# Attention and two mixture-of-experts layers in one kernel: two weight halves are split at other places, and the last block is scaled by one engine

## The chip, the cores and the metric

The kernel runs on one core of a Trainium2 chip. The metric is the device time of one execution in microseconds (us), the median of several runs. The engines are named as the profile names them: PE is TensorE's matmuls and PEld its weight loads, DVE is VectorE, ACT is ScalarE, POOL is GpSimd, SP is the queue that issues most of the loads.

## What is computed

A decayed linear attention gives 1536 rows of 512. These go through a first layer of eight experts, in which each row is used only if a skip score is positive and whose result is added to the row, and then through a second layer of eight experts with a capacity. Each layer picks one expert for each row by the largest logit, applies two matrices with a ReLU between them, and scales by the softmax weight:

```python
def reference(**kwargs):
    ...
    attn_out = _attn_ref(**attn_kwargs)
    B, H, S, D = attn_out.shape
    x = np.ascontiguousarray(attn_out.transpose(0, 2, 1, 3)).reshape(B * S, H * D)
    x = _moe_ref(x=x, **moe_kwargs)
    return _moe2_ref(x=x, **moe2_kwargs)

def _moe_ref(x, w_skip, w_gate, w1, w2):
    ...
        h = np.maximum(xc[mask] @ w1[e], 0.0)
        y[mask] = gate_w[mask, None] * (h @ w2[e])
    out[do_compute] = xc + y

def _moe2_ref(x, w_gate, w1, w2, capacity):
    ...
    h = np.maximum(np.einsum('ecd,edf->ecf', disp, w1), 0.0)
    y = np.einsum('ecf,efd->ecd', h, w2)
    ...
            out[i] = gate_w[i] * y[expert_idx[i], pos[i]]
```

## The kernel before

**Products and weights.** A product of float32 matrices is made from three products of rounded parts: a tensor x is split into hi, x rounded to the type fp32r, and lo = x − hi, rounded likewise; hi·hi, hi·lo and lo·hi are summed (`mm3`, `mm3s`, lines 803 to 811). The weights come from DRAM as float32, in chunks of 1 MB (half a matrix of an expert), into five raw buffers named big. A chunk is split in two halves of 128x1024: for each half ScalarE makes hi (line 258) and VectorE lo (line 261). With the second half the raw buffer goes back to a list of free ones, and the next chunk can be loaded into it from SP's queue (line 219); SP's load waits for the last reader of the buffer, which is VectorE's subtraction. Weights of the first layer are w1a and w2a, of the second w1b and w2b.

**How the order is set.** The program's order on each engine is the order in which the Python code emits it. Generators emit a layer piece by piece. Between the pieces the code calls `step_side`, which first lets the routing generators take a step and then calls `pump(1, pieces[0])`: `pump` raises a counter of turns, emits up to `pieces[0]` weight halves (each with its ScalarE and its VectorE instruction), if a loaded chunk and a place for it are there, and then issues the loads for which buffers are free. So `pieces[0]` says how many halves are split at a step.

**The first layer and its picks.** For each expert e the code emits layer 1 (`layer1`: products into s, ReLU at line 834 into h), turns h by transposes on TensorE (line 782) with the rounding on ScalarE (line 387, hTh) and the remainder on VectorE (line 388, hTl), and runs layer 2 of the expert before it (`layer2`, products into o). `result` (line 866) scales that expert's accumulator and adds the row on VectorE, which makes its rows for the second layer ("row"). The rows are then routed by `route_b`, for the experts 0 to 5 in couples, for 6 and for 7 alone: transposes on TensorE (line 887), logits (lines 892 and 898), the pick on VectorE (`pick`: the maximum mx at line 307, d, t, tm and the mask m at line 323, with ScalarE's exponential ex at line 315), ranks by two products of the mask (lines 335 and 336), slot and one-hot row on VectorE (lines 918, 920 and 924), and eight or four products into the slot table tab (line 349). The third couple is that of experts 4 and 5.

**Between the layers.** Beside layer 1 of the second layer's expert 0 the rows of expert 7 are routed (the generator `last`; its steps are called at i = 2, 4, 5, 8 and 12 of the loop from line 1084). Then VectorE casts the slot table to indices (line 1094, ids_b), and POOL issues five indirect gathers of 128 rows each by these indices (`load_block`, line 371). The first of them, block (0, 1), is turned on TensorE at line 782 amid layer 2 of expert 0.

**The second layer and the end.** Expert 0 has its two blocks one at a time, experts 1 to 7 two blocks of 128 rows as a pair (`pair_layer1`, `pair_layer2`). `emit_out` scales a block's accumulator by the softmax weight into y, and POOL scatters y to the output rows (line 941). For the very last block the work of the scaling is shared: ScalarE takes columns 0 to 255 (line 936) and VectorE columns 256 to 511 (line 938). All other blocks are scaled by ScalarE alone.

Of the kernel before, what the change touches and what calls it, by code (L numbers as in the profile page):

```python
# [11 lines left out]
ACTF = mybir.ActivationFunctionType  # L12
ALU = mybir.AluOpType
# [3 lines left out]
NT, DM, E, FF = B * S, H * D, 8, 1024  # L17
# [7 lines left out]
GCOL, IDCOL = DM, DM + 2  # L25
# [16 lines left out]
def kernel(  # L42
# [12 lines left out]
    nc = tc.nc  # L55
# [136 lines left out]
    def whole(kind, e, j):  # L192

        return kind == "w2a" and e in (1, 3) and j == 1
# [72 lines left out]
    def used(key, h):  # L267
        if key not in whole_keys:
            w_free.append((count["turn"] + 2, held.pop((key, h))))
        elif h:  # L270
            raw_free.append((0, held.pop(key)))
# [4 lines left out]
    def pump(n, pieces):  # L276

        count["turn"] += 1
        for _ in range(pieces):
            if not splitting:  # L280
                if not ready():
                    break
                splitting.append(split_half(n))
            try:
                next(splitting[0])
            except StopIteration:
                splitting.clear()
        load_w()
# [77 lines left out]
    def gather(at, n=None, t=None):  # L366

        n = n or done[0]
        if t is None:
            t = xs_free.pop(0)  # L370
        nc.gpsimd.indirect_dma_start(
            out=t, out_offset=None, in_=table[0:n, :], in_offset=bass.IndirectOffsetOnAxis(ap=at, axis=0),
            bounds_check=n - 1, oob_is_err=False,
        )
        return t
# [386 lines left out]
    def psum(tag="t", bufs=3):  # L762
        return ps.tile([128, 512], F32, tag=tag, bufs=bufs, name=tag)
# [43 lines left out]
    def mm3s(acc, pairs, first, last):  # L807

        todo = [(a[0], w[i]) for a, w in pairs for i in range(2)] + [(a[1], w[0]) for a, w in pairs]
        for i, (a, w) in enumerate(todo):  # L810
            nc.tensor.matmul(out=acc, lhsT=a, rhs=w, start=first and i == 0, stop=last and i == len(todo) - 1)  # L811
            if i % 2 and i < len(todo) - 1:
                yield

    def at_k(parts, *ix):
        return tuple(t[(slice(None),) + ix] for t in parts)

    def layer1(x, kind, e, parts=None, fine=False):

        h = m_p.tile([128, FF], F32, tag="h", name="h", bufs=1)  # L820
        for j in range(2):
            acc = psum("s", 2)
            for k in (0, 2):
                w = wt[kind, e, j][k // 2]
                for _ in mm3s(acc, [(at_k(x, k + i), at_k(w, i)) for i in range(2)], k == 0, k == 2):
                    if fine:
                        yield
                if done_with(kind, e):
                    used((kind, e, j), k // 2)
                if not k:  # L830
                    if j and parts is not None:
                        parts.append(turned(h, 0, "hT"))
                    yield
            nc.scalar.activation(out=h[:, 512 * j:512 * j + 512], in_=acc, func=ACTF.Relu)
            yield
        return h

    def layer2(hT, kind, e):
        acc = psum("o", 2)
        for k in range(0, FT, 2):  # L840
            w = wt[kind, e, k // 4]
            a = hT[k // 4]
            h, k0 = k % 4 // 2, k % 4
            if whole(kind, e, k // 4):
                for i in (k0, k0 + 1):
                    nc.tensor.matmul(out=acc, lhsT=a[0][:, i, :], rhs=w[:, i, :], start=k + i == 0, stop=k == FT - 2 and i == 3)  # L846
            else:
                for _ in mm3s(acc, [(at_k(a, k0 + i), at_k(w[h], i)) for i in range(2)], k == 0, k == FT - 2):
                    pass
            if done_with(kind, e):  # L850
                used((kind, e, k // 4), h)
            yield
        return acc
# [4 lines left out]
    def done_with(kind, e):  # L858
        if (kind, e) not in (("w1b", 0), ("w2b", 0)):
            return True  # L860
        return uses.get(kind, 0) > 0
# [68 lines left out]
            to_slots(where[i], rhs[:, i], 8, 8)  # L930
        yield

    def emit_out(xs, acc, shared=False):
        y = m_p.tile([128, DM], F32, tag="y", name="y")
        n = DM // 2 if shared else DM
        nc.scalar.activation(out=y[:, 0:n], in_=acc[:, 0:n], func=ACTF.Copy, scale=xs[:, GCOL + 1:GCOL + 2])  # L936
        if shared:
            nc.vector.tensor_scalar(out=y[:, n:DM], in0=acc[:, n:DM], scalar1=xs[:, GCOL + 1:GCOL + 2], scalar2=None, op0=ALU.mult)
        ix = sm.tile([128, 1], I32, tag="ixo", name="ixo")
        nc.gpsimd.tensor_scalar(out=ix, in0=xs[:, IDCOL:IDCOL + 1], scalar1=4096.0, scalar2=None, op0=ALU.add)  # L940
        new = nc.gpsimd.indirect_dma_start(  # L941
            out=out[:, :], out_offset=bass.IndirectOffsetOnAxis(ap=ix, axis=0), in_=y, in_offset=None,
            bounds_check=NT - 1, oob_is_err=False,
        )
        for old in written:
            tc.declare_no_dep(new.ins, old.ins, reason="rows of other tokens")
        written.append(new)
        if xs is not a0:
            xs_free.append(xs)
# [18 lines left out]
    pieces = [1]  # L968
# [9 lines left out]
    def step_side():  # L978
        for g in list(side):
            try:  # L980
                next(g)
            except StopIteration:
                side.remove(g)
        pump(1, pieces[0])

    def run(gen):

        while True:
            try:
                next(gen)  # L990
            except StopIteration as stop:
                return stop.value
            step_side()
# [5 lines left out]
    def last_step(gen, n):  # L999

        for i in range(n):
            next(gen)
            if i < n - 1:
                step_side()
        try:
            next(gen)
        except StopIteration as stop:
            return stop.value
# [23 lines left out]
    acc = run(second)  # L1032
    then_route(0, acc)
    for e in range(1, E):
        first = layer1(x, "w1a", e)
        if e == 1:
            for _ in range(2):
                next(first)
                step_side()
            x = turned(xs1[2], 0, "x")  # L1040
        h = run(first)
        if e + 4 < E:
            xs1[e + 4] = gather(ids[:, e + 4:e + 5], 1 + NT)
        elif e == 4:
            gather(ids[:, 8:9], 1 + NT, a0)
        turn = split_T(h, FT, "hT", (True, not whole("w2a", e, 1)))
        if e > 1:
            second = layer2(hT.pop(e - 1), "w2a", e - 1)
            next(second)
            step_side()  # L1050
            site()
            x = turned(xs1[e + 1] if e + 1 < E else a0, 0, "x")
            if e == E - 1:

                for _ in range(2):
                    next(second)
                    step_side()
                    site()
                    next(turn)
            acc = last_step(second, FT // 2 - (3 if e == E - 1 else 1))  # L1060
            then_route(e - 1, acc, step_side)
        if e < E - 1:
            site()
        hT[e] = run(turn)
    side += sited
    second = layer2(hT.pop(E - 1), "w2a", E - 1)
    for i in range(FT // 2):
        next(second)
        pieces[0] = i < 2
        if i < FT // 2 - 1:  # L1070
            step_side()
    acc = run(second)
# [4 lines left out]
    xs2 = {(0, 0): a0}  # L1077

    def load_block(e, j):
        xs2[e, j] = gather(ids_b[:, 8 * j + e:8 * j + e + 1])  # L1080
# [3 lines left out]
    for i in range(1, 13):  # L1084
        next(first)
        if i % 3 == 0:
            step_side()
        if i in (2, 4, 5, 8, 12):
            next(last)
# [4 lines left out]
    nc.vector.tensor_copy(out=ids_b, in_=tab[:, 8:24])  # L1094
    for e, j in ((0, 1), (1, 0), (1, 1), (2, 0), (2, 1)):
        load_block(e, j)
    second = layer2(h0, "w2b", 0)
    next(second)
    h0.append(turned(h, 1, "hT"))
# [4 lines left out]
    acc = run(second)  # L1104
# [44 lines left out]
    def pair_layer2(hs, e):  # L1149
        acc = [psum("o", 2), psum("o", 2)]  # L1150
        for c in range(2):
            w = wt["w2b", e, c]
            for j in range(2):
                for k in range(4):
                    mm3(acc[j], at_k(hs[c], k, slice(128 * j, 128 * j + 128)), at_k(w[k // 2], k % 2), c + k == 0, c + k == 4)
                if c:
                    emit_out(xs2[e, j], acc[j], e == E - 1 and j > 0)
                for h in range(2 * j):
                    used(("w2b", e, c), h)
                step_side()  # L1160
# [11 lines left out]
    acc = run(second)  # L1172
# [207 lines left out]
```

## Time and profile before

| | |
|---|---|
| median of 3 runs (lowest, highest) | 386.19 us (384.45, 387.62) |
| the profiled execution | 386.53 us |
| its span in the profile | 384.5 us |
| PE busy | 370.6 us, 96% of the span |
| PEld busy | 313.4 us, 82% |
| DVE busy | 244.2 us, 64% |
| ACT busy | 214.0 us, 56% |
| POOL busy | 116.0 us, 30% |

A span begins with the first instruction and ends with the last event that the profiler saw; all times of day in this document are microseconds from the span's start. An engine's instructions run in its program's order. "Idle before" is the time that an engine stood still ahead of an instruction, and the name behind the arrow is what ended that. The matmuls are pipelined, one begins before the modelled end of the one ahead, so a PE wait can be read by the distance of starts as well as by the idle time.

### The profile page before, as it was taken

The numbers are of one execution on the slowest core, as the hardware profiler recorded it, in microseconds if no ns is written. First come the engines' busy times: TensorE is split into PE (matmuls) and PEld (weight loads), VectorE is DVE, ScalarE is ACT, GpSimd is POOL, SyncE is SP. The second block draws the span as 40 slices with busy tenths as digits, with TensorE's granted clock in tenths as the row PEclk, the third lists the DMA queues.
The fourth block names the chain that finished last, engine by engine and source line by source line (L and its number), as shares of the span: only waits on it lengthen the run. The fifth ranks groups of instructions, "written<-read, shape, count | busy, mean of one in ns | idle before, by whom it ended". The sixth has DMA issues, their size and how long they took to land.

```text
span 384.5 us, 6806 instructions
## 1 busy us (share of the span) xinstructions
PE 370.6 (96%) x2641; PEld 313.4 (82%) x2641; DVE 244.2 (64%) x402; ACT 214.0 (56%) x317; POOL 116.0 (30%) x185
## 2 busy tenths in 40 slices
PE   8999999699999999999999999999999999999992
PEld 4788887688867778886678998989989898998981
DVE  3557776649998889799626983646727476373200
ACT  1446554458979668796337773547536454562100
POOL 3677773274130040142252401305032040401102
PEclk9999999789999999999999999999999999999997
DMA  8999876499999999898835784956749387110101
GB/s 297 415 421 400 355 222 219 113 412 350 414 411 402 334 360 331 298 310 318 294 116 162 263 338 134 313 195 202 267 146 331 112 263 267 54 51 14 41 2 45
DMA packets 18944, 95.99 MB, mean 250 GB/s; under 512 B 3217, under 2 KB 3473, under 8 KB 9432
## 3 DMA queue, kind: packets, MB, share of 16 engines
q1 hardware_dynamic: 13012, 80.86, 57.0%
q0 software_dynamic: 3280, 9.76, 8.0%
q10 hardware_dynamic: 2612, 4.86, 3.4%
q8 instruction: 23, 0.38, 0.4%
q14 instruction: 17, 0.14, 0.1%
HBM read 87.03 MB, written 9.48 MB: 251 GB/s over the span
## 4 chain that ended last, share of the span: by engine, by line
PE 88%; DVE 5%; ACT 3%; issue 2%; DMA 1%; POOL 0%; POOLq 0%; DVEq 0%; ACTq 0%
PE s L811 14%; PE o L811 9%; PE s L805 7%; PE s L804 7%; PE s L803 7%; PE o L805 7%; PE o L803 7%; PE o L804 7%; PE m L691 3%; PE s L641 3%; DVE lo L261 3%; PE t L782 3%; PE m L682 3%; PE o L846 2%; PE t L1121 2%
## 5 line engine op out<-in xcount | busy, mean ns | idle before, releaser
L261 DVE TENSOR_TENSOR lo<-big,hi 128x1024 fp32r<-128x1024 f32 (+1 forms) x130 | 151.1, 1184 | 58.2 <-ACT hi L258 57.7
L258 ACT ACTIVATE hi<-big 128x1024 fp32r<-128x1024 f32 (+1 forms) x130 | 128.0, 1014 | 2.9 <-DMA big<-in_w1a_dram 1.2
L805 PE MATMUL s<-xh,lo 128*128 128x256 f32 x224 | 63.4, 283 | 0.0
L804 PE MATMUL s<-xl,hi 128*128 128x256 f32 x224 | 63.4, 283 | 0.0
L803 PE MATMUL s<-xh,hi 128*128 128x256 f32 x224 | 63.4, 283 | 0.0
L941 POOL DMA_INDIRECT out_dram<-y,ixo x16 | 18.6, 1165 | 138.4 <-ACT y L936 136.8
L803 PE MATMUL o<-hi,hTh 128*128 128x512 f32 x112 | 44.2, 394 | 0.0
L805 PE MATMUL o<-hi,hTl 128*128 128x512 f32 x112 | 43.6, 390 | 0.0
L804 PE MATMUL o<-lo,hTh 128*128 128x512 f32 x112 | 43.6, 389 | 0.0
L804 PEld LDWEIGHTS s<-xl,hi 128*128 128x128 f32 x224 | 43.0, 192 | 0.3
L803 PEld LDWEIGHTS s<-xh,hi 128*128 128x128 f32 x224 | 43.0, 192 | 0.3
L805 PEld LDWEIGHTS s<-xh,lo 128*128 128x128 f32 x224 | 43.0, 192 | 0.0
L1140 ACT ACTIVATE hTh<-s 128x512 fp32r<-128x512 f32 x28 | 16.8, 598 | 39.0 <-PE s L805 39.0
L1141 DVE SCALAR_TENSOR_TENSOR hTl<-s,hTh 128x512 fp32r<-128x512 f32 x28 | 19.3, 690 | 28.4 <-ACT hTh L1140 28.4
L936 ACT ACTIVATE y<-o,rowc 128x512 f32<-128x512 f32 (+1 forms) x15 | 10.1, 675 | 45.3 <-issue 29.3
L811 PE MATMUL s<-hi,xh 128*128 128x512 f32 x80 | 33.4, 417 | 0.7 <-DVE xl L388 0.7
L811 PE MATMUL s<-lo,xh 128*128 128x512 f32 x80 | 32.0, 400 | 0.0
L811 PE MATMUL o<-hi,hTh 128*128 128x512 f32 x72 | 29.7, 412 | 0.0
L811 PE MATMUL o<-lo,hTh 128*128 128x512 f32 x72 | 28.2, 391 | 0.0
L811 PE MATMUL s<-hi,xl 128*128 128x512 f32 x80 | 25.4, 400 | 0.0
L805 PEld LDWEIGHTS o<-hi,hTl 128*128 128x128 f32 x112 | 21.0, 188 | 4.5
L804 PEld LDWEIGHTS o<-lo,hTh 128*128 128x128 f32 x112 | 21.1, 188 | 4.2
(162 smaller groups left out, 601.6 us busy)
## 6 DMA issues: line engine op xcount, KB each, us to landing
big<-in_w1a_dram SPq DMA_DIRECT2D x16, 1024.0 KB, 6.9
big<-in_w2a_dram SPq DMA_DIRECT2D x16, 1024.0 KB, 7.2
big<-in_w1b_dram SPq DMA_DIRECT2D x16, 1024.0 KB, 5.1
big<-in_w2b_dram SPq DMA_DIRECT2D x16, 1024.0 KB, 5.8
qk<-in_qkv_dram SPq DMA_DIRECT2D x5, 1024.0 KB, 8.4
big<-in_qkv_dram SPq DMA_DIRECT2D x5, 1024.0 KB, 8.4
table<-rowc ACTq DMA_DIRECT2D x4, 516.0 KB, 7.1
table<-row ACTq DMA_DIRECT2D x3, 516.0 KB, 5.3
```

The costliest lines, as they stand in the source:

```text
L258: nc.scalar.activation(out=hi[:, k], in_=r3[:, k], func=ACTF.Copy)
L261: nc.vector.tensor_tensor(out=lo[:, k], in0=r3[:, k], in1=hi[:, k].bitcast(F32), op=ALU.subtract)
L641: nc.tensor.matmul(out=sa[j][:, 128 * r:128 * r + 128], lhsT=kk[64 * j:64 * j + 64, r, :], rhs=q[64 * j:64 * j + 64, r, :], start=True, st ...
L682: nc.tensor.matmul(out=o[:, 128 * r:128 * r + 128], lhsT=sbd[c % 2][:, b, r, :], rhs=q[:, r, :], start=r == 0, stop=False, skip_group_chec ...
L691: nc.tensor.matmul(out=o[64 * j:64 * j + 64, 128 * r:128 * r + 128], lhsT=v[:, b, 2 * r + j, :], rhs=pt[c, b][j][:, r, :], start=not c and ...
L803: nc.tensor.matmul(out=acc, lhsT=a[0], rhs=w[0], start=first, stop=False)
L804: nc.tensor.matmul(out=acc, lhsT=a[0], rhs=w[1], start=False, stop=False)
L805: nc.tensor.matmul(out=acc, lhsT=a[1], rhs=w[0], start=False, stop=last)
L811: nc.tensor.matmul(out=acc, lhsT=a, rhs=w, start=first and i == 0, stop=last and i == len(todo) - 1)
L941: new = nc.gpsimd.indirect_dma_start(out=out[:, :], out_offset=bass.IndirectOffsetOnAxis(ap=ix, axis=0), in_=y, in_offset=None, bounds_che ...
L1140: nc.scalar.activation(out=hi[:, g:g + 2, :], in_=acc, func=ACTF.Relu)
L1141: nc.vector.scalar_tensor_tensor(out=lo[:, g:g + 2, :], in0=acc, scalar=0.0, in1=hi[:, g:g + 2, :].bitcast(F32), op0=ALU.max, op1=ALU.subtract
```

## The change

Three edits. In the iteration of the last first-layer expert, the two steps ahead of the row of expert 6 split one half and none, where they split one each; the step right behind that row splits two, where it split one. In the loop over layer 2 of expert 7, the steps split one half only at i = 0, where they did at i = 0 and 1; the half left over is split at the step of i = 9 of the loop in which expert 7's rows are routed. The last block is scaled by ScalarE over all 512 columns. The number of halves is the same, and so is their sequence.

```diff
-    def emit_out(xs, acc, shared=False):
+    def emit_out(xs, acc):
         y = m_p.tile([128, DM], F32, tag="y", name="y")
-        n = DM // 2 if shared else DM
-        nc.scalar.activation(out=y[:, 0:n], in_=acc[:, 0:n], func=ACTF.Copy, scale=xs[:, GCOL + 1:GCOL + 2])
-        if shared:
-            nc.vector.tensor_scalar(out=y[:, n:DM], in0=acc[:, n:DM], scalar1=xs[:, GCOL + 1:GCOL + 2], scalar2=None, op0=ALU.mult)
+        nc.scalar.activation(out=y, in_=acc, func=ACTF.Copy, scale=xs[:, GCOL + 1:GCOL + 2])
...
             if e == E - 1:
-                for _ in range(2):
+                for pieces[0] in (1, 0):
                     next(second)
                     step_side()
                     site()
                     next(turn)
+                pieces[0] = 2
             acc = last_step(second, FT // 2 - (3 if e == E - 1 else 1))
             then_route(e - 1, acc, step_side)
...
     for i in range(FT // 2):
         next(second)
-        pieces[0] = i < 2
+        pieces[0] = i < 1
...
     for i in range(1, 13):
         next(first)
         if i % 3 == 0:
+            pieces[0] = i == 9
             step_side()
         if i in (2, 4, 5, 8, 12):
             next(last)
...
     for e, j in ((0, 1), (1, 0), (1, 1), (2, 0), (2, 1)):
         load_block(e, j)
+    pieces[0] = 0
     second = layer2(h0, "w2b", 0)
...
-                    emit_out(xs2[e, j], acc[j], e == E - 1 and j > 0)
+                    emit_out(xs2[e, j], acc[j])
```

The first place is on VectorE, at the pick of experts 4 and 5 (mx to m). In the piece of the difference, hTl is the remainder of the turned h of expert 7, and big_87 and big_89 are raw buffers of second-layer weights.

```order
 L261 TENSOR_TENSOR lo<-big_89,hi 128x1024
 L388 TENSOR_TENSOR hTl<-t,hTh 128x4x128
-L261 TENSOR_TENSOR lo<-big_87,hi 128x1024
 L307 TENSOR_REDUCE mx<-t 128x2
 L310 TENSOR_TENSOR d<-t,mx 128x16
```

One half, the first of big_87, is gone from between hTl and the pick.

The second place is on VectorE again, from the row of expert 6 (line 866) to the pick of expert 6 (the second mx); between them stand the slots and one-hot rows of experts 4 and 5 (lines 918 to 924).

```order
 L388 TENSOR_TENSOR hTl<-t,hTh 128x4x128
 L866 SCALAR_TENSOR_TENSOR row_1186<-o,rowc_106 128x512
-L261 TENSOR_TENSOR lo<-big_87,hi 128x1024
+L261 TENSOR_TENSOR lo<-big_87,hi 128x1024 x2
 L918 TENSOR_TENSOR prb<-t,m 128x16
 L920 TENSOR_REDUCE slb<-prb 128x2
 L924 TENSOR_SCALAR whereb<-iota,slb 128x257 x2
-L261 TENSOR_TENSOR lo<-big_88,hi 128x1024 x2
+L261 TENSOR_TENSOR lo<-big_88,hi 128x1024
 L307 TENSOR_REDUCE mx<-t 128x1
 L310 TENSOR_TENSOR d<-t,mx 128x8
```

Behind the row both halves of big_87 stand now, and ahead of expert 6's pick only one half of big_88.

The third place is the end of expert 7's routing, on VectorE: whereb is its one-hot row, hTl the remainder of the first half of h of the second layer's expert 0, and ids_b the indices for the gathers.

```order
 L924 TENSOR_SCALAR whereb<-iota,slb 128x257
 L388 TENSOR_TENSOR hTl<-t,hTh 128x4x128
+L261 TENSOR_TENSOR lo<-big_88,hi 128x1024
 L1094 CAST ids_b<-tab 128x16
 L388 TENSOR_TENSOR hTl<-t,hTh 128x4x128
```

The second half of big_88 now stands between hTl and the cast. On ScalarE the same place reads before (the ReLUs at line 834 make the two halves of h):

```order
L364 DMA table<-row_1186 128x516
L834 ACTIVATE h<-s 128x512
L387 ACTIVATE hTh<-t 128x4x128
L834 ACTIVATE h<-s 128x512
L387 ACTIVATE hTh<-t 128x4x128
```

and now:

```order
L364 DMA table<-row_1186 128x516
L834 ACTIVATE h<-s 128x512
L387 ACTIVATE hTh<-t 128x4x128
L258 ACTIVATE hi<-big_88 128x1024
L834 ACTIVATE h<-s 128x512
```

The rounding of that half stands behind the first hTh and ahead of the second ReLU. The order on SP is the same as before; its load into big_88 waits, as before, for the subtraction of that buffer's second half.

## Rows read from the trace of the kernel before

**Rows 1.** Stages: length, busy PE, PEld, DVE, ACT, POOL; granted clock; DMA share; GB/s.
```profile
187.00:212.00 25.00, 24.84 (x148) 19.53 (x149) 12.05 (x29) 12.16 (x19) 9.21 (x18) 1.00 0.53 168
...
212.00:374.00 162.00, 162.00 (x1057) 148.73 (x1056) 88.97 (x102) 80.34 (x106) 31.18 (x36) 1.00 0.51 176
```

**Rows 2.** Timeline, PE, 162 to 188: start, us, line, operation, count, idle before, releaser.
```profile
162.64 0.61 PE L811 MATMUL o<-hi,hTl 128*128 128x512 f32 x2
...
163.10 0.18 PE L335 MATMUL t<-m,lc 128*128 128x16 bf16 x1
...
179.53 0.61 PE L811 MATMUL o<-hi,hTl 128*128 128x512 f32 x2
...
181.07 0.63 PE L887 MATMUL t<-cs,row 128*128 128x128 f32 x4 [0.93 <-DVE row L866]
...
186.14 0.62 PE L811 MATMUL o<-hi,hTl 128*128 128x512 f32 x2
...
187.13 0.18 PE L335 MATMUL t<-m,lc 128*128 128x8 bf16 x1 [0.37 <-DVE m L323]
```

**Rows 3.** Timeline, DVE, 180 to 196, same columns.
```profile
180.18 0.74 DVE L866 SCALAR_TENSOR_TENSOR row<-o,rowc 128x512 f32<-128x512 f32 x1
...
183.38 1.23 DVE L261 TENSOR_TENSOR lo<-big,hi 128x1024 fp32r<-128x1024 f32 x1 [0.38 <-ACT hi L258]
...
184.89 1.23 DVE L261 TENSOR_TENSOR lo<-big,hi 128x1024 fp32r<-128x1024 f32 x1 [0.28 <-ACT hi L258]
...
186.03 0.16 DVE L307 TENSOR_REDUCE mx<-t 128x1 f32<-128x8 f32 x1
...
195.65 0.17 DVE L1094 CAST ids_b<-tab 128x16 int32<-128x16 f32 x1 [0.32 <-PE tab L349]
```

**Rows 4.** Timeline, ACT, 178 to 195.
```profile
178.83 0.58 ACT L387 ACTIVATE hTh<-t 128x512 fp32r<-128x512 f32 x1
...
179.31 1.05 ACT L258 ACTIVATE hi<-big 128x1024 fp32r<-128x1024 f32 x1
...
194.00 0.60 ACT L387 ACTIVATE hTh<-t 128x512 fp32r<-128x512 f32 x1 [0.75 <-PE t L782]
```

**Rows 5.** Line 371, first gather behind the cast: on POOL, and its landing.
```profile
196.10 1.11 POOL L371 DMA_INDIRECT rowc<-table,ids_b  x1 [2.54 <-DVE ids_b L1094]
...
DMA to landing us min/median/max: 3.6/3.6/3.6
```

**Rows 6.** Timeline, PEld, 198 to 211: weights for that block's transposes.
```profile
199.91 0.59 PEld L782 LDWEIGHTS t<-cs,rowc 128*128 128x128 f32 x4
```

**Rows 7.** Loads on SP: that of 186.15; landing of that of 207.96.
```profile
186.15 0.33 SPq L219 DMA_DIRECT2D big<-in_w1b_dram  x1
...
big<-in_w1b_dram SPq DMA_DIRECT2D x1, 1024.0 KB, 4.8
```

**Rows 8.** Loads on SP and a gather on POOL, 72 to 90; that gather's landing.
```profile
77.21 8.04 SPq L219 DMA_DIRECT2D big<-in_w2a_dram  x2
...
77.67 1.09 POOL L371 DMA_INDIRECT rowc<-table,ids  x1 [7.59 <-DVE lo L261]
...
DMA to landing us min/median/max: 7.1/7.1/7.1
```

**Rows 9.** PE at 71.50, and the stretch 72.40 to 79.10 (columns as rows 1).
```profile
71.50 1.35 PE L381 MATMUL m<-cs,a 128*128 128x128 f32 x8 [2.10 <-DMA a<-table,ids]
...
72.40:79.10 6.70, 5.96 (x28) 5.04 (x27) 2.26 (x4) 1.71 (x3) 1.12 (x2) 0.50 0.83 251
```

**Rows 10.** Timeline, ACT, DVE and POOL, 374 to 385: the last two blocks.
```profile
374.64 0.69 ACT L936 ACTIVATE y<-o,rowc 128x512 f32<-128x512 f32 x1 [7.64 <-PE o L805]
...
377.36 0.47 ACT L936 ACTIVATE y<-o,rowc 128x256 f32<-128x256 f32 x1 [2.03 <-PE o L805]
...
377.87 0.48 DVE L938 TENSOR_SCALAR y<-o,rowc 128x256 f32<-128x256 f32 x1 [10.14 <-ACT y L936]
...
379.13 1.05 POOL L941 DMA_INDIRECT out_dram<-y,ixo  x1 [1.69 <-DVE y L938]
```

## The prediction, made before the changed kernel ran

> **What bounds the kernel now.** I read the table of stages first. From 187 on TensorE is the engine that sets the pace: busy 24.84 of 25.00 us up to 212, and 162.00 of 162.00 from there to 374, at the full granted clock [rows 1]. So a microsecond by which TensorE stops between 180 and 212 comes back in none of the stages behind it; it stands in the end time. The second view was the chain of waits: it runs along TensorE nearly everywhere and leaves it for VectorE and ScalarE between 157 and 187, where the last two picks of the first layer's results are made. The third view was the timeline of each engine around the two places that the change touches, then the end.
>
> Three places matter. At 181.07 TensorE has stood still for 0.93 us for expert 6's row on VectorE, and at 187.13 for 0.37 us for the mask of expert 6's pick [rows 2]. At 195.65 VectorE casts the slot list to indices, 0.32 us after it had run out of work [rows 3]; POOL issues the first of five gathers at 196.10, and its 128 rows land 3.6 us later, at 199.70 [rows 5]. TensorE begins to load these rows as weights at 199.91, without having waited [rows 6]. That gather has at most 0.21 us to spare.
>
> **The change part by part.** The sum is made against the profiled execution: 386.53 us, that is its span of 384.5 and 2.03 around it. The median of the three runs, 386.19, lies 0.34 below; I add the differences to the median.
>
> *The half taken from ahead of the couple's pick.* VectorE loses one subtraction of about 1.2 us ahead of the pick of experts 4 and 5, so that pick comes earlier. Nobody on the path wants it earlier: expert 6's row starts at 180.18, and its accumulator is complete at 179.53 + 0.61 = 180.14 [rows 2, 3]. TensorE sets that row, so the 0.93 us stays. I cost this at nothing; it could cost up to one subtraction only if VectorE were late for the row, and it now has less to do ahead of it.
>
> *The same half, behind expert 6's row.* Between that row and the pick of expert 6 VectorE has three weight halves before and three after, only others. But before, it waited for ScalarE ahead of two of them, 0.38 and 0.28 us [rows 3]; now the first two are rounded by ScalarE early, and one is left behind the turned row. The pick can therefore start up to 0.66 us before 186.03. TensorE's wait for its mask was 0.37 us; by the starts it is 0.53: where the same rank product follows its pair without a wait, it starts 0.46 us behind the pair's start (162.64, 163.10), here 0.99 (186.14, 187.13) [rows 2]. I take the 0.53, since 0.66 covers it. TensorE, and all that follows it, is earlier by **0.53 us** from 187 on. Bounds: 0 if another input of the pick is as late, 0.53.
>
> *The half put into the last rank's pause.* It stands on ScalarE behind the rounding of the first half of h, and on VectorE between its remainder and the cast. The pause on VectorE is the 0.32 us ahead of the cast; the half doesn't fit into it. Step by step, with TensorE 0.53 earlier: that rounding starts at 194.00 − 0.53 = 193.47; the next on ScalarE follows 0.48 behind it (178.83, 179.31) and takes 1.05 [rows 4]; VectorE's subtraction then starts, and what stands behind it follows 1.14 us later (184.89, 186.03) [rows 3]. The cast comes at 193.47 + 0.48 + 1.05 + 1.14 = 196.14 instead of 195.65. Behind it wait POOL's five gathers, behind the first of them TensorE's transposes of that block, and behind these the rest of the program in TensorE's order. The gather is issued 0.45 us behind the cast (195.65, 196.10), at 196.59 [rows 3, 5].
>
> *What goes to the queue with it.* The buffer of that weight comes free with its second half. Before, SP loaded it again at 186.15 [rows 7], right behind the subtraction at 184.89 + 1.23 = 186.12 [rows 3], and 10 us ahead of the gathers. Now the subtraction ends at 195.00 + 1.23 = 196.23 and the 1 MB load starts at 196.26, 0.33 us ahead of the gather that TensorE is about to wait for. The weight itself is wanted much later; the collision is the cost. The gather's landing has these bounds: 3.6 us as it had alone [rows 5], and 7.1 us as the gather of 77.67 had it, issued 0.46 us behind a load but with two more unfinished ahead [rows 8]. Here there is one load, and one load alone lands 4.8 us from its issue [rows 7]. I take it that the gather lands with the load: 196.26 + 4.8 = 201.06, which is 4.5 us after its own issue and nearer to the row of 3.6 than to that of 7.1. That is 201.06 − 199.70 = **1.36 us later** than before, the 0.53 already in it. By the bounds the shift is 196.59 + 3.6 − 199.70 = 0.49 up to 196.59 + 7.1 − 199.70 = 3.99. TensorE would stand still from 199.91 − 0.53 = 199.38 to 199.91 + 1.36 = 201.27, 1.9 us.
>
> *The last block.* ScalarE scaled one half in 0.47 us and VectorE the other in 0.48, and these ran one behind the other: 377.36, then 377.87 to 378.35; POOL's scatter started at 379.13, 0.78 behind [rows 10]. One instruction over 512 columns took 0.69 for the block before (374.64) [rows 10]. So the scatter can start 0.78 behind 377.36 + 0.69 = 378.05, at 378.83: **0.30 us gained**, with nothing behind it but the scatter's landing. Bounds 0 and 0.30.
>
> Sum: + 1.36 − 0.30 = + 1.06 us: 387.6 against the profile, **387.2 us** against the median.
>
> **The rivals.**
>
> *The gather isn't held up by the load.* The gather then lands after 3.6 us, and the sum is + 0.49 − 0.30 = + 0.2: 386.4 us. For it speaks that it is only 128 rows beside 1 MB and could have its turns in between; against it, 7.1 us behind a load [rows 8]. The Trainium skill's page "DMA: Bandwidth & Descriptors" (Queues, rings and completion order) says that each DMA engine goes round its queues packet by packet. By that rule a gather, in POOL's queue, need not wait until SP's load is through, and the time is this rival's; the gather of 77.67 speaks against it.
>
> *TensorE's stop costs it its clock.* This is the slower side. At 71.50 TensorE had stood still 2.10 us for a gather, and from 72.40 to 79.10 the granted clock was 0.50, the 1.2 GHz level [rows 9]: 6.7 us at half speed, 3.35 us lost. Stops of 0.93 and 0.37 at 181.07 and 187.13 [rows 2] left it at 1.00 in the stretch behind them [rows 1]. It decides from a stop between 0.93 and 2.10 on; mine, 1.9, lies near the upper one, in the middle of the dense second stage. Price: 387.2 + 3.35 = 390.6 us. Against it: before 71.50 the work was small products, here it is dense on both sides.
>
> *Nothing is late.* If the half fits after all (the cast first by some slack that I don't see, or a landing that came well ahead of 199.70), only the gains stay: − 0.53 − 0.30 = − 0.83, 385.4 us. Rows 6 give 0.21 us of slack, so little speaks for it.
>
> **How the numbers follow.** My forecast (late gather, full clock) has 0.42, the loss of clock 0.25, the gather undisturbed 0.25, nothing late 0.08. A measurement of this kernel tells about 1%, 3.9 us, from no change. Slower by that is the loss of clock and a rest of landings near 7.1: 0.26. Faster by over 1% is out of reach of all cases: 0.02 for what I don't see. Within 1%: 0.72. The likeliest case's own range is 386.4 to 389.5. The whole range reaches down to the case in which nothing is late, 385.2, and up to the loss of clock with a landing somewhat above 4.5 us, 391.2.
>
> **What would show it.** Right: no wait of TensorE for the mask at 187; the cast some 0.5 us later than 195.65; SP's load at about 196.3, next to the first gather, whose landing takes over 4 us; TensorE idle 1 to 2.5 us ahead of the transposes at line 782; one scaling of 0.69 us at the end. Wrong: the wait for the mask still there (then another input was late), no idle time of TensorE ahead of those transposes, or a gather that lands in 3.6 us beside the load. A granted clock of 0.50 somewhere between 200 and 210 would show the slower rival.

## The result, and the profile after

The changed kernel took 387.53 us in the median of 21 runs (384.87 to 390.31), the kernel before 385.07 in 21 runs beside it (383.14 to 389.72). The ratio is 1.0061 with a 95% interval of 1.0039 to 1.0083: slower by 2.4 us (1.5 to 3.2). The forecast was 387.2 us, 1.0 more than the median known then, a ratio of 1.0027. The move is within 1%, to the side that was forecast, and larger than forecast.

The two spans, 384.5 us and 385.1, can't be compared as they stand. The kernel before had its stretch at half clock early in the profiled execution [rows 9]; the changed kernel, in its own, had none there, only a shorter one of some 3.4 us from 8.7 on, and was 2.07 us ahead (161.03 against 163.10) at a rank product that the change doesn't touch. So I measure from that product on, in five parts, each from the start of one instruction of TensorE to the start of the next. For the kernel before the first three marks are in [rows 2], the last scatter in [rows 10]; the two marks missing there are the first transposes of block (0, 1) and the last product (timeline of PE, start and duration in us first):

```profile
200.14 0.60 PE L782 MATMUL t<-cs,rowc 128*128 128x128 f32 x4
...
376.88 0.39 PE L805 MATMUL o<-hi,hTl 128*128 128x512 f32 x1
```

The same marks in the changed kernel, with the pair that ends just ahead of each wait, which is the engine's timeline again (the brackets give the idle time before and what ended it):

```profile
161.03 0.18 PE L335 MATMUL t<-m,lc 128*128 128x16 bf16 x1
...
177.46 0.62 PE L811 MATMUL o<-hi,hTl 128*128 128x512 f32 x2
...
178.46 0.63 PE L887 MATMUL t<-cs,row 128*128 128x128 f32 x4 [0.39 <-DVE row L866]
...
184.00 0.18 PE L335 MATMUL t<-m,lc 128*128 128x8 bf16 x1
...
196.58 0.61 PE L811 MATMUL o<-hi,hTl 128*128 128x512 f32 x2
...
199.47 0.80 PE L782 MATMUL t<-cs,rowc 128*128 128x128 f32 x4 [2.28 <-DMA rowc<-table,ids_b]
...
377.78 0.39 PE L805 MATMUL o<-hi,hTl 128*128 128x512 f32 x1
```

| part, us | before | after | difference |
|---|---|---|---|
| rank product to expert 6's row transposed (163.10 to 181.07; 161.03 to 178.46) | 17.97 | 17.43 | −0.54 |
| to expert 6's rank product (187.13; 184.00) | 6.06 | 5.54 | −0.52 |
| to the transposes of block (0, 1) (200.14; 199.47) | 13.01 | 15.47 | +2.46 |
| to the last product (376.88; 377.78) | 176.74 | 178.31 | +1.57 |
| to the last scatter (379.13; 379.72) | 2.25 | 1.94 | −0.31 |
| sum | 216.03 | 218.69 | +2.66 |

The sum agrees with the 2.4 us of the timed runs. Three parts gained 1.37 us, two lost 4.03.

The third part holds the cause. On VectorE of the changed kernel the half stands between hTl and the cast:

```profile
176.96 0.69 DVE L388 TENSOR_TENSOR hTl<-t,hTh 128x512 fp32r<-128x512 f32 x1 [0.51 <-ACT hTh L387]
...
177.57 0.74 DVE L866 SCALAR_TENSOR_TENSOR row<-o,rowc 128x512 f32<-128x512 f32 x1
...
191.51 0.69 DVE L388 TENSOR_TENSOR hTl<-t,hTh 128x512 fp32r<-128x512 f32 x1 [1.12 <-ACT hTh L387]
...
192.45 1.23 DVE L261 TENSOR_TENSOR lo<-big,hi 128x1024 fp32r<-128x1024 f32 x1 [0.26 <-ACT hi L258]
...
193.60 0.17 DVE L1094 CAST ids_b<-tab 128x16 int32<-128x16 f32 x1
```

The cast doesn't wait for the slot table any longer, as it did in [rows 3]; it waits behind the half. What follows it are SP's load into the freed buffer, the first gather on POOL and, in the chain of waits, the time until that gather had landed (start, us):

```profile
193.71 0.33 SPq L219 DMA_DIRECT2D big<-in_w1b_dram  x1
...
194.04 1.11 POOL L371 DMA_INDIRECT rowc<-table,ids_b  x1 [3.60 <-DVE ids_b L1094]
...
194.04 5.30 DMA rowc<-table,ids_b
```

The load starts 0.33 us ahead of the gather, which lands after 5.30 us; without the load it had taken 3.6 [rows 5]. The fourth part is the price of the clock behind the stop that this makes. The stretches there, in the changed kernel (columns as in rows 1; the granted clock is the third figure from the end):

```profile
199.00:200.00 1.00, 0.53 (x5) 0.56 (x5) 0.00 (x0) 0.00 (x0) 0.70 (x2) 0.90 1.07 388
200.00:201.00 1.00, 1.00 (x5) 0.81 (x4) 0.07 (x1) 0.60 (x1) 0.61 (x2) 0.50 0.78 231
201.00:202.00 1.00, 1.00 (x4) 0.81 (x3) 0.63 (x1) 0.00 (x0) 0.00 (x0) 0.50 0.61 182
202.00:203.00 1.00, 1.00 (x5) 0.48 (x5) 0.06 (x1) 0.13 (x1) 0.00 (x0) 0.50 0.28 107
203.00:204.00 1.00, 1.00 (x5) 0.82 (x6) 0.12 (x1) 1.00 (x2) 0.00 (x0) 0.89 0.00 0
```

From late in the first of them to early in the last the granted clock was 0.50, the 1.2 GHz level, for some 3.4 us (0.2 + 3 + 0.2), in which the work of 1.7 us was done; TensorE had stood still for 2.28 us before. The end (timelines of ACT and POOL) shows the one scaling and the scatter behind it:

```profile
378.25 0.69 ACT L935 ACTIVATE y<-o,rowc 128x512 f32<-128x512 f32 x1 [2.03 <-PE o L805]
...
379.72 1.05 POOL L938 DMA_INDIRECT out_dram<-y,ixo  x1 [1.38 <-ACT y L935]
```

### The profile page after: what moved, and what is told of

Read it like the earlier page. It is cut to its first block, busy times and chain, and to the rows that moved or that the text cites. A ratio compares the mean times of both kernels' runs of the same rounds, so it can differ in the third digit from the quotient of the medians.

```text
span 385.1 us, 6803 instructions
## 1 busy us (share of the span) xinstructions
PE 368.6 (96%) x2641; PEld 312.0 (81%) x2641; DVE 243.9 (63%) x401; ACT 214.2 (56%) x317; POOL 119.0 (31%) x185
## 4 chain that ended last, share of the span: by engine, by line
PE 86%; DMA 7%; ACT 2%; issue 2%; DVE 1%; SPq 0%; ACTq 0%; POOL 0%; POOLq 0%; DVEq 0%
PE s L811 12%; PE o L811 11%; PE s L805 7%; PE s L804 7%; PE s L803 7%; PE o L805 7%; PE o L803 7%; PE o L804 7%; PE m L691 3%; PE t L782 3%; PE s L641 3%; PE m L682 3%; DMA rowc<-table,ids 2%; PE o L846 2%; PE t L1122 2%
## 5 line engine op out<-in xcount | busy, mean ns | idle before, releaser
L935 ACT ACTIVATE y<-o,rowc 128x512 f32<-128x512 f32 x15 | 10.3, 689 | 45.4 <-issue 29.3
```

## The experiments

Each kernel was timed against the kernel before in five rounds on the chip, unless said otherwise; the five parts come from one profiled execution of it. Here are the parts of all of them, in us, as differences to the kernel before:

| kernel | to row 6 | to mask 6 | to block (0, 1) | to last product | to last scatter | sum | timed ratio (95%) |
|---|---|---|---|---|---|---|---|
| changed kernel | −0.54 | −0.52 | +2.46 | +1.57 | −0.31 | +2.66 | 1.0061 (1.0039 to 1.0083) |
| 1: half one pause earlier | −0.54 | −0.53 | 0.00 | +0.01 | −0.31 | −1.37 | 0.9985 (0.9955 to 1.0014) |
| 2: load held | −0.54 | −0.53 | +0.63 | +0.01 | −0.31 | −0.74 | 1.0002 (0.9974 to 1.0031) |
| 3: cast first | −0.54 | −0.53 | +0.01 | 0.00 | −0.30 | −1.36 | 0.9974 (0.9944 to 1.0004) |
| 4: before, load late | 0.00 | −0.01 | +1.84 | +0.03 | 0.00 | +1.86 | 1.0064 (1.0030 to 1.0098) |
| 5: filler products | −0.54 | −0.53 | +2.49 | +0.03 | −0.30 | +1.15 | 1.0027 (0.9996 to 1.0058) |
| 6: pick alone | −0.54 | +0.28 | +0.02 | 0.00 | 0.00 | −0.24 | not timed |
| 3 again | −0.54 | −0.51 | +0.01 | 0.00 | −0.31 | −1.35 | 0.9961 (0.9932 to 0.9990) |

Every interval holds the sum of its kernel's parts. Only three leave out 1: those of the changed kernel, of experiment 4 and of the second timing of experiment 3. For the others the parts carry the argument.

**1. The half one pause earlier.** Against the changed kernel:

```diff
         if i % 3 == 0:
-            pieces[0] = i == 9
             step_side()
...
     result(E - 1, xs1[E - 1], acc)
+    pieces[0] = 1
     step_side()
+    pieces[0] = 0
```

> The changed kernel, with the half of the last rank's pause split one pause earlier: right behind expert 7's row, so on ScalarE ahead of the turned row of expert 7 and on VectorE ahead of expert 7's pick, where VectorE stood idle for 2.3 us; nothing new stands ahead of the cast, and the load into that buffer starts some 7 us ahead of the gathers. Theory (the loss is the gather that comes late and lands beside the load, with the clock that the stop costs): the first gather lands 3.6 us from its issue, TensorE doesn't wait for it, its granted clock stays at 1.00 there, and the three gains stay: 0.54 at expert 6's row, 0.52 at its mask, 0.31 at the end, about 1.4 us less than the kernel before, a ratio of 0.996. Rival one (the loss is the scaling of the last block by one engine, or the pick's new neighbours): the time stays as that of the changed kernel, a ratio of 1.006. Rival two (the half costs its place wherever it stands): expert 7's pick and with it the cast are late by about 1 us, TensorE waits for the gather some 0.5 to 1 us, a ratio of 1.000.

The third and fourth parts are back to nothing and the gains stay. The row of the stretch and the cast:

```profile
196.00:204.00 8.00, 8.00 (x42) 6.41 (x41) 2.90 (x4) 4.42 (x7) 4.26 (x6) 1.00 0.51 156
...
192.14 0.17 DVE L1095 CAST ids_b<-tab 128x16 int32<-128x16 f32 x1 [0.33 <-PE tab L349]
```

TensorE is busy for 8.00 of 8.00 us at a clock of 1.00, and the cast waits for the slot table again, for 0.33 us. Both rivals fall: the last block is scaled by one engine here too, and a half costs nothing in the earlier pause. The timed interval holds the expected 0.996 and leaves out the 1.006 of rival one. It holds the 1.000 of rival two as well, so that one falls by the profile alone.

**2. The load held.** Against the changed kernel (`hold` is a scratch tile in DRAM; the small store stands in SP's queue ahead of the load):

```diff
             pieces[0] = i == 9
+            kept[0] = 99 if i == 9 else kept[0]
             step_side()
...
     pieces[0] = 0
+    hold = dram.tile([1, 4], F32, name="hold")
+    nc.sync.dma_start(out=hold, in_=xs2[0, 1][0:1, 0:4])
+    kept[0] = 0
+    load_w()
```

> The changed kernel, with the half ahead of the cast as it is, but SP's load into that buffer queued behind a small store of 16 bytes that needs the first gather's rows, so that the load can't start before that gather has landed. It parts the two halves of the loss. Theory (the load is the larger part): the cast stays 0.5 us late against TensorE's order, the first gather lands after 3.6 us in place of 5.3, TensorE waits 0.6 us in place of 2.3, and the clock stays at 1.00: about 0.8 us less than before, a ratio of 0.998. Rival (the load is harmless, the gather is slow for its own sake or for the late cast alone): the gather still lands after 5 us, TensorE waits 2 us and more, a ratio of 1.006.

The timelines of PE and SP:

```profile
198.32 0.63 PE L782 MATMUL t<-cs,rowc 128*128 128x128 f32 x4 [0.47 <-DMA rowc<-table,ids_b]
...
198.54 0.34 SPq L219 DMA_DIRECT2D big<-in_w1b_dram  x1
```

The cast is as late as in the changed kernel, but TensorE waits 0.47 us instead of 2.28, the third part is 0.63 longer than before instead of 2.46, and no clock is lost. So of the 2.46 us the load beside the gather makes 1.83, the late cast 0.63. The timed interval holds the expected 0.998 and leaves out the rival's 1.006.

**3. The cast first.** Against the changed kernel:

```diff
         if i % 3 == 0:
-            pieces[0] = i == 9
             step_side()
...
         load_block(e, j)
+    pump(1, 1)
     pieces[0] = 0
```

> The changed kernel, with the same half right behind the cast and the five gathers in the order instead of ahead of the cast; the load into its buffer then starts about 1 us behind the first gather's issue. Theory: the cast is 1.1 us earlier against TensorE's order than in the changed kernel, the gather is partly through when the load's data begins, and lands after 3.6 to 4.6 us; TensorE waits 0 to 1 us for it, without loss of clock: 0.4 to 1.4 us less than before, a ratio of 0.996 to 0.999. Rival (a load that starts behind a gather holds it up just as one that starts ahead): landing after 5.3 us, TensorE waits about 1.2 us, a ratio of 1.000.

The timelines of POOL, SP and PE:

```profile
192.26 1.11 POOL L371 DMA_INDIRECT rowc<-table,ids_b  x1 [2.54 <-DVE ids_b L1093]
...
194.54 0.33 SPq L219 DMA_DIRECT2D big<-in_w1b_dram  x1
...
196.30 0.60 PE L782 MATMUL t<-cs,rowc 128*128 128x128 f32 x4
```

The load starts 2.28 us behind the gather's issue (I had written about 1) and TensorE doesn't wait at all. Measured a second time, unchanged:

> The kernel with the half behind the cast and the gathers once more, unchanged, for a narrower interval against the kernel before: by the parts of its profile it is 1.36 us shorter from the pick of experts 4 and 5 to the end, a ratio of 0.9965. The rival is no difference, 1.000.

In this second profile the load starts 2.28 us behind the gather's issue again, and line 371 has the landing of that gather:

```profile
DMA to landing us min/median/max: 3.4/3.4/3.4
```

The second ratio, 0.9961 (0.9932 to 0.9990), has 1 outside its interval. With its parts of −1.36 and −1.35 us this version beats both kernels, and a load that starts so late did the gather no harm.

**4. The kernel before, with the load late.** Against the kernel before:

```diff
         pieces[0] = i < 2
+        kept[0] = 99 if i else kept[0]
         if i < FT // 2 - 1:
...
     nc.vector.tensor_copy(out=ids_b, in_=tab[:, 8:24])
+    hold = dram.tile([1, 2], I32, name="hold")
+    nc.sync.dma_start(out=hold, in_=ids_b[0:1, 0:2])
+    kept[0] = 0
+    load_w()
```

> The kernel before, with one load moved alone: SP's load into the buffer freed ahead of expert 6's pick is queued behind a small store of 8 bytes that needs the cast indices, so that it starts at about 195.9, 0.2 us ahead of the first gather, in place of 186.15. No half moves and the last block stays shared. Theory: the first gather lands 1 to 1.8 us later than the 3.6 us that it had, TensorE, which had almost no time to spare, waits that long, and may lose clock behind it: 1 to 1.8 us more than before, with loss of clock up to 5, a ratio of 1.003 to 1.013. Rival (the load's neighbourhood is harmless): no wait of TensorE at those transposes, a ratio of 1.000.

The timelines of SP, POOL and PE, and the stretch around:

```profile
195.47 0.34 SPq L219 DMA_DIRECT2D big<-in_w1b_dram  x1
...
195.38 1.11 POOL L371 DMA_INDIRECT rowc<-table,ids_b  x1 [2.56 <-DVE ids_b L1095]
...
201.23 0.63 PE L782 MATMUL t<-cs,rowc 128*128 128x128 f32 x4 [1.65 <-DMA rowc<-table,ids_b]
...
196.00:204.00 8.00, 6.35 (x34) 4.85 (x33) 1.56 (x3) 1.90 (x4) 4.73 (x6) 1.00 0.87 296
```

Apart from the store of 8 bytes only the time of one load changed, and TensorE waits 1.65 us that it didn't wait before (the store alone wasn't tried). The load started 0.09 us behind the gather here, not ahead of it as I had meant, and held it up all the same. The clock stayed at 1.00 behind this stop of 1.65 us.

**5. Filler products.** Against the changed kernel:

```diff
+    warm(psum(), 10)
     x = turned(xs2[0, 1], 0, "x")
```

> The changed kernel, with ten products of zeros over 512 columns on TensorE (2.2 us) ahead of the transposes that wait for the first gather, so that TensorE doesn't stand still there. Theory (the stop of 2.3 us costs the clock on top of itself): the transposes start as late as in the changed kernel, but the granted clock stays at 1.00 behind them and the 1.57 us that the 176.74 us from there to the last product had grown by are gone: a ratio to the kernel before of 1.002 to 1.004 in place of 1.006. Rival (the clock fell for another reason, or its fall cost little in most runs): a stretch at 0.50 behind the transposes as before, a ratio of 1.006 or, with the products in the way, more.

The timeline of PE (it has nine of the ten products) and the stretch behind:

```profile
197.75 2.33 PE L567 MATMUL t<-zb 128*128 128x512 bf16 x9
...
200.21 0.63 PE L782 MATMUL t<-cs,rowc 128*128 128x128 f32 x4
...
197.00:204.00 7.00, 6.83 (x33) 4.38 (x34) 0.93 (x3) 2.24 (x3) 3.60 (x6) 1.00 0.78 282
```

The transposes start as late as in the changed kernel (part three +2.49), but the clock stays at 1.00 and part four is back at +0.03. So the 1.57 us of part four came with the stretch at half clock, and where the stop was filled that stretch is gone. That the stop brought it is likely but rests on one profile of each kernel; a stop of this length doesn't always cost the clock (experiment 6's profile has one, shown below under the loss of clock). The timed ratio, 1.0027, stands where it was expected; its interval overlaps that of the changed kernel, so for the size in the timed runs it is a hint, not a proof.

**6. The pick alone.** One profiled execution, not timed in rounds. Against the kernel before:

```diff
             if e == E - 1:
-                for _ in range(2):
+                for pieces[0] in (1, 0):
                     next(second)
                     step_side()
                     site()
                     next(turn)
+                pieces[0] = 2
```

> The kernel before, with the first edit alone: the half goes from ahead of the couple's pick to behind expert 6's row; the halves behind that row stay as they were, so four stand there instead of three; the last block stays shared. Theory (the row of expert 6 waited for VectorE, not for TensorE): TensorE's wait for that row falls from 0.93 to 0.39 us as in the changed kernel; the fourth half makes expert 6's mask late, so that wait is some 0.9 us in place of 0.37. Together about 0.1 us less than before. Rival (the row is set by its accumulator, as the prediction had it): the wait for the row stays at 0.93 us.

```profile
179.57 0.63 PE L887 MATMUL t<-cs,row 128*128 128x128 f32 x4 [0.39 <-DVE row L866]
...
185.91 0.18 PE L335 MATMUL t<-m,lc 128*128 128x8 bf16 x1 [0.65 <-DVE m L323]
```

The timeline of PE has the wait for expert 6's row at 0.39 us without any other edit, so it was VectorE that set the row in the kernel before. The fourth half makes the mask late: its wait grows from 0.37 to 0.65 us, less than the 0.9 that I had expected. The first edit alone brings 0.24 us; only with the half put elsewhere does it bring 1.06.

## Why the prediction was right, and where it was not

**The half taken from ahead of the pick: wrong.** The step that failed is "TensorE sets that row, so the 0.93 us stays. I cost this at nothing". It gained 0.54 us. I had taken the pair of 179.53 as the last of expert 6's accumulator. In the changed kernel the row starts at 177.57, while the pair that stands in the same place, at 177.46, runs until 178.08: the row can't have needed it. By the order of the code that pair ends the first group of expert 7's layer 2. Expert 6's accumulator was complete one group earlier, in the kernel before at 178.15 + 0.62 = 178.77, 1.4 us ahead of its row (the timeline of all engines, kernel before):

```profile
178.15 0.62 PE L811 MATMUL o<-hi,hTl 128*128 128x512 f32 x2
178.30 0.17 DVE L307 TENSOR_REDUCE mx<-t 128x2 f32<-128x16 f32 x1
...
179.58 0.69 DVE L388 TENSOR_TENSOR hTl<-t,hTh 128x512 fp32r<-128x512 f32 x1
```

The row started at 180.18 [rows 3] behind hTl on VectorE, and hTl behind the pick, without a pause; now hTl waits for ScalarE's hTh, 0.51 us, and that is the next limit. Experiment 6 shows the 0.54 by itself.

**The half behind the row: right.** 0.53 us was forecast, 0.52 measured, and TensorE's wait for the mask is gone.

**The half in the last rank's pause: right.** The cast was to come 0.49 us later, with TensorE 0.53 earlier, that is 1.02 later against TensorE's order. Against the slot products that it needs it moved by 1.05 (195.35 to 195.65 before, 192.25 to 193.60 after: 0.30 and 1.35 us). These products on PE, first in the kernel before, then in the changed one:

```profile
195.35 0.26 PE L349 MATMUL tab<-rhsb,whereb 128*128 128x8 bf16 x4
...
192.25 0.26 PE L349 MATMUL tab<-rhsb,whereb 128*128 128x8 bf16 x4
```

**The load that goes with it: right in kind, too small.** The load was forecast 0.33 us ahead of the gather, and so it came. The mis-sized term is the landing: I took 4.5 us, the profile has 5.30. TensorE was to be held up by 1.36 + 0.53 = 1.89 us; it was 2.46. The landing itself moved further: from expert 6's rank product on it came after 12.57 us before (187.13 to 199.70) and 15.34 in the changed kernel (184.00 to 199.34), 2.77 us later. Some 0.3 us of that went into the time that the gather had had to spare, which the prediction had put at 0.21 at most and hadn't taken off. Experiments 2 and 4 part the load's share from the cast's, 1.83 and 0.63.

**The gather not held up by the load: fell.** That rival had a chance of 0.25. In the changed kernel the load, had it taken its 4.8 us [rows 7], would have been through at 198.5, and the gather landed at 199.34, behind that. That trace has no landing for the load; in experiment 5, where it starts 0.34 us ahead of the gather, it has one:

```profile
big<-in_w1b_dram SPq DMA_DIRECT2D x1, 1024.0 KB, 5.0
```

So the load came hardly later than those 4.8 us, and most of the delay fell on the gather. The Trainium skill's page "DMA: Bandwidth & Descriptors" (Queues, rings and completion order) says that each DMA engine takes its queues in turn, packet by packet. No trace here shows single packets; the 3.6 us that I drew from that rule for a gather behind a load didn't come.

**The loss of clock: happened, at half its price.** I gave it 0.25 and 3.35 us, from the 6.7 us at half clock of [rows 9]. The profiled execution had some 3.4 us at 0.50 and lost 1.57 us. In this execution, then, the slower rival came true and not the forecast's own case of a full clock.

The point from which a stop costs the clock was put between 0.93 and 2.10 us. The stretch behind the 0.93, 181 to 187, isn't in [rows 1]; its clock was 1.00 as well. A stop of 1.65 us kept the clock in experiment 4, one of 2.28 didn't in the changed kernel; but the length of the stop doesn't settle it. In experiment 6 TensorE stood still for 2.42 us where the kernel before stood for 2.10 [rows 9], and kept its clock (timeline of PE; stretch with columns as in rows 1):

```profile
71.89 1.16 PE L381 MATMUL m<-cs,a 128*128 128x128 f32 x8 [2.42 <-DMA a<-table,ids]
...
72.00:90.00 18.00, 16.08 (x90) 13.32 (x91) 12.06 (x14) 12.17 (x16) 8.99 (x11) 1.00 0.87 322
```

At the same place stops of 2.27 us (experiment 5) and 2.33 (experiment 3 again) were followed by some 3.4 us at 0.50. And the changed kernel fell to 0.50 at 8.7, near its start, with stops of only 0.32 and 0.62 us:

```profile
7.73 0.46 PE L641 MATMUL s<-qk 64*128 64x128 f32 x2 [0.32 <-PE s L641]
8.81 1.44 PE L641 MATMUL s<-qk 64*128 64x128 f32 x10 [0.62 <-DVE mask L592]
...
9.00:10.00 1.00, 1.00 (x10) 1.00 (x12) 0.86 (x2) 0.00 (x0) 1.00 (x2) 0.50 1.22 407
```

What decides it stays open. How many of the timed runs lost the clock behind the gather isn't shown by these profiles either.

**The last block: right.** 0.30 us was forecast, 0.31 measured, in every kernel with this edit and in none without.

So the forecast's sum, +1.06, held errors of opposite sign: a gain of 0.54 that I had ruled out, a loss of 0.57 too little at the gather, and 1.57 in the clock that I had left to a rival. 1.06 − 0.54 + 0.57 + 1.57 = 2.66, which is what the parts show. Without the loss of clock it would be 1.09, nearly the forecast (experiment 5 has 1.15), but by luck: the first two errors cancel. The late gather, the wait and their side of the sum were foreseen. The upper end of the likeliest range, 389.5, lies below what its own bound of 7.1 us gives: 386.19 + 3.99 − 0.30 = 389.9.

## What to carry to other kernels

A piece of work fits into an engine's pause only if it ends before the pause does: 0.32 us stood ahead of the cast, 2.3 us one pick earlier, and the same half cost 2.46 us, and in the profiled execution the clock, in the one and nothing in the other. Work that frees a buffer moves a transfer as well: look at what that transfer will stand beside, above all beside a gather with no time to spare. Before saying which engine sets an instruction, make sure from the code which products its accumulator needs, since groups of one shape follow each other without a mark in the trace.

## What was not expected of the hardware

One load of 1 MB lengthened a gather of 128 rows from 3.6 us to 5.30 when it was issued 0.33 us ahead, and stopped TensorE for 1.65 us when it was issued 0.09 us behind the gather; issued 2.28 us behind, it cost nothing, and the gather landed after 3.4. And a stop of TensorE has no fixed price: one of 2.10 us was followed by 6.7 us at half clock [rows 9], those of 2.27, 2.28 and 2.33 by some 3.4, and one of 2.42 by none.
